# SyncE instead of GpSimd gathers the engines and clears the semaphores at the end of a decode kernel

## The chip, the cores and the metric

The kernel runs on one core of a Trainium2 chip. The metric is the device time of one execution in microseconds (us), as the median of several executions. "Relative to the copy" below means relative to the start of the last ScalarE instruction, which copies the finished output from PSUM; this takes the chance in the 379 us before it (some tenths of a microsecond from run to run) out of the comparison.

## The reference

One decode step of a gated mixture: grouped-query attention over a cache of 65,536 positions, a gMLP mixer for one token, and a gate between them.

```python
g = sigmoid((x * gate_w).sum(-1, keepdims=True))      # x: (1, 1, 1024) bf16
# a: 32 query heads, 4 kv heads, k_cache and v_cache (1, 4, 65536, 128) bf16, projections wq and wo
# b: gelu(x @ w_in), split, layernorm of one half, product, @ w_out
out = g * a + (1 - g) * b
```

Only the size matters to what follows: 162 MB must be read from HBM once, and the output is 2 KB.

## The kernel before

The body streams the caches through SBUF. The change does not touch it. What it touches is a function that rewrites the program's last block when the program is finished. The language's standard ending is a barrier of all engines, a clear of the kernel's semaphores by GpSimd, and a second barrier. The function had already cut this down to one gathering. After it the block is, engine by engine:

```text
TensorE, VectorE, ScalarE, SyncE:  drain, add 1 to the gather semaphore (96)
GpSimd:  five waits for two semaphores each (all loads and all engines' work done)
         drain (with an eleventh wait); wait until the gather is 4, subtract 4; drain; clear semaphores 100 to 111; drain
SyncE (after its own drain):  wait until the output has landed (semaphore 99 >= 32), subtract 32
```

The code that does it, cut:

```python
if engine == mybir.EngineType.Pool:
    drop += [l[2][0], l[6][0], l[7][0]]
    closer, gather = l[0][0], l[1][2]          # closer: the drain that gets the waits
    continue
...                                            # SyncE's waits are taken to hand them to closer
drop += [l[1][0], l[2][0]]
if engine == mybir.EngineType.SP:
    closed = l[3][0]                           # SyncE's last wait: for the output
else:
    drop.append(l[3][0])
...
block.instructions[closer] = copy.replace(
    block.instructions[closer],
    sync_info=mybir.SyncInfo(on_wait=list(waits.values()), on_update=[]))
```

The output itself is copied by ScalarE and written in two halves, one issued by ScalarE and one by SyncE:

```python
nc.scalar.copy(out=out_sb[:], in_=out_ps[:])
for i, queue in enumerate((nc.scalar, nc.sync)):
    p0 = (2 * i + 1) * B - 1
    ins = queue.dma_start(out=out_rows[2 * i:2 * i + 2, :], in_=out_sb[p0:p0 + 2, :])
    out_queues.append(ins.ins.name)
```

Of the kernel before, what the change touches and what calls it, by code (L numbers as in the profile page):

```python
# [29 lines left out]
def kernel(  # L30
# [90 lines left out]
    def close_with_one_barrier(n):  # L121
        block = n.main_func.blocks[-1]
        by = {}
        for i, ins in enumerate(block.instructions):
            by.setdefault(ins.engine, []).append((i, type(ins).__name__, ins))
        drop = []
        waits = None
        for engine, l in by.items():
            kinds = [k for _, k, _ in l]
            if engine == mybir.EngineType.Pool:  # L130
                assert kinds == ["InstDrain", "InstEventSemaphore", "InstEventSemaphore",
                                 "InstDrain", "InstISA", "InstDrain", "InstEventSemaphore",
                                 "InstEventSemaphore"]
                drop += [l[2][0], l[6][0], l[7][0]]
                closer, gather = l[0][0], l[1][2]
                continue
            if engine == mybir.EngineType.SP:
                assert l[0][2].has_wait() and not l[0][2].has_update()
                waits = list(l[0][2].sync_info.on_wait)
                drop.append(l[0][0])  # L140
                l, kinds = l[1:], kinds[1:]
            assert kinds == ["InstDrain", "InstEventSemaphore"] * 2
            drop += [l[1][0], l[2][0]]
            if engine == mybir.EngineType.SP:
                closed = l[3][0]
            else:
                drop.append(l[3][0])
        waits = {w.id: w for w in waits}
        total = 0
        for b in n.main_func.blocks:  # L150
            for i, ins in enumerate(b.instructions):
                if ins.name in out_queues:
                    u, = ins.sync_info.on_update
                    w = waits[u.id]
                    waits[u.id] = copy.replace(w, wait_value=w.wait_value - u.update_value)
                    total += u.update_value
                    b.instructions[i] = copy.replace(ins, sync_info=mybir.SyncInfo(
                        on_wait=ins.sync_info.on_wait,
                        on_update=[copy.replace(u, id=landed.num, ant_name=landed.name)]))
# [3 lines that stand above are left out]
        w, u = gather.sync_info.on_wait[0], gather.sync_info.on_update[0]  # L163
        block.instructions[closed] = copy.replace(
            block.instructions[closed],
            sync_info=mybir.SyncInfo(
                on_wait=[copy.replace(w, id=landed.num, ant_name=landed.name, wait_value=total)],
                on_update=[copy.replace(u, id=landed.num, ant_name=landed.name,
                                        update_value=total)]))
        for i in sorted(drop, reverse=True):  # L170
            del block.instructions[i]

    nc.at_finalize(close_with_one_barrier)

    kv = big.tile([P, NKV * CT * P], BF16, name="kv")
# [377 lines left out]
# [3 lines that stand above are left out]
# [40 lines left out]
```

## Time and profile before

| | |
|---|---|
| time, median of 3 runs | 382.19 us (382.17 to 382.25) |
| span of the profile, first to last instruction | 380.65 us |
| DMA busy, HBM rate over the span | 99%, 426 GB/s |
| start of the output copy to the end of the span | 1.73 us |
| end of the span to the end of the time | 1.51 us |

The page of the profile: busy time by engine, the busy share of 40 slices (9 is 90% or more), and the start of the chain that ended last.

```profile
PE 233.2 (61%) x1395; PEld 56.0 (15%) x800; DVE 218.5 (57%) x211; ACT 39.6 (10%) x55; POOL 4.4 (1%) x10
...
POOL 4000000000000000000000000000000000000000
...
DMA  9998999999999999999999999999999999999995
...
DMA 57%; PE 26%; DVE 13%; ACT 2%; issue 1%; SPq 1%; DVEq 0%; ACTq 0%
```

Only the first slice of GpSimd (POOL) has work: its set-up. DMA is full in nearly every slice but the last, whose 9.5 us hold the tail. So the kernel's length is set by the stream of loads, and an edit of the ending can change only the last two or three microseconds.

The tail by time (start us, duration us, engine, line, operation):

```profile
378.58 0.29 PE L506 MATMUL out_ps<-kv,oa 128*32 128x256 bf16 x4 [0.35 <-DMA kv<-in_A_wo_dram]
...
378.92 0.37 ACT L552 CAST out_sb<-out_ps 128x256 bf16<-128x256 f32 x1 [45.10 <-PE out_ps L506]
379.32 0.32 SPq L555 DMA_DIRECT2D out_dram<-out_sb  x1
379.32 0.25 ACTq L555 DMA_DIRECT2D out_dram<-out_sb  x1
```

The timeline stops here because waits, drains and clears are not counted as work. They appear when one asks for the line of the program's end. These are its groups before (line, engine, operation, count: duration in ns min/median/max, first and last start in us):

```profile
L591 POOLq EVENT_SEMAPHORE  x6: 17/43/682, 376.0 to 379.9; - x6
L591 POOLq DRAIN  x3: 34/41/72, 379.4 to 380.2; - x3
...
L591 SPq DRAIN  x1: 174/174/174, 379.7 to 379.7; - x1
L591 POOLq EVENT_SEMAPHORE_RANGE_CLEAR  x1: 96/96/96, 380.1 to 380.1; - x1
L591 SPq EVENT_SEMAPHORE  x1: 17/17/17, 380.6 to 380.6; - x1
```

GpSimd gathers and clears between 379.9 and 380.2, and SyncE's last wait stands at 380.6, when the output lands. Read like this, GpSimd looks hidden. But the time runs on for 1.51 us after the span. What happens there is in the trace's record of semaphore updates: the runtime's own end of a program. The Trainium skill, "Runtime: NRT & Kernel Launch", section "The ~15µs preamble/postamble breakdown", describes it: a barrier, then each engine resets 51 semaphores, then a barrier again; for the barrier at the start it also gives the pass, through the five engines and back. The trace agrees, and shows that pass at the end too. Semaphore 2 is raised nine times, semaphores up to 255 are reset in five blocks side by side, and semaphore 2 is raised nine times more:

```text
before: raises of semaphore 2, us from the span's start
first barrier   379.178 380.015 380.758 380.802 380.825 | 380.922 380.961 380.995 381.042
second barrier  381.919 381.953 381.992 382.035 382.058 | 382.157 382.195 382.229 382.276
```

The nine are five engines in a fixed order and then four on the way back, each waiting for the one before it. The ninth raise releases the block of resets that ends last (semaphores 51 to 101). So what moves the ninth raise moves the end. The reported time (382.16 us in this profile) is the distance from the last such raise at the start of the program to the sixth raise of the second barrier: 382.161 us.

### The profile page before, as it was taken

The numbers are of one execution on the slowest core, as the hardware profiler recorded it, in microseconds if no ns is written. First come the engines' busy times: TensorE is split into PE (matmuls) and PEld (weight loads), VectorE is DVE, ScalarE is ACT, GpSimd is POOL, SyncE is SP. The second block draws the span as 40 slices with busy tenths as digits, with TensorE's granted clock in tenths as the row PEclk, the third lists the DMA queues.
The fourth block names the chain that finished last, engine by engine and source line by source line (L and its number), as shares of the span: only waits on it lengthen the run. The fifth ranks groups of instructions, "written<-read, shape, count | busy, mean of one in ns | idle before, by whom it ended". The sixth has DMA issues, their size and how long they took to land.

```text
span 380.7 us, 2605 instructions
## 1 busy us (share of the span) xinstructions
PE 233.2 (61%) x1395; PEld 56.0 (15%) x800; DVE 218.5 (57%) x211; ACT 39.6 (10%) x55; POOL 4.4 (1%) x10
## 2 busy tenths in 40 slices
PE   0060657876157944796397729871977196839386
PEld 0010101111101210111011101120211011202113
DVE  4133288997597506966977059669970388460040
ACT  1001001110601100114010001050100000500000
POOL 4000000000000000000000000000000000000000
PEclk9995769899759895989688958895989579969789
DMA  9998999999999999999999999999999999999995
GB/s 386 496 420 379 411 438 441 437 483 430 387 420 441 441 436 441 427 441 441 434 436 441 441 427 434 406 423 441 434 434 429 420 441 442 436 410 430 424 443 223
DMA packets 3943, 162.17 MB, mean 426 GB/s; under 512 B 472, under 2 KB 476, under 8 KB 860
## 3 DMA queue, kind: packets, MB, share of 16 engines
q1 hardware_dynamic: 3892, 162.01, 98.8%
q8 instruction: 8, 0.13, 0.1%
q14 instruction: 3, 0.02, 0.0%
q10 hardware_dynamic: 40, 0.01, 0.0%
HBM read 162.01 MB, written 0.00 MB: 426 GB/s over the span
## 4 chain that ended last, share of the span: by engine, by line
DMA 57%; PE 26%; DVE 13%; ACT 2%; issue 1%; SPq 1%; DVEq 0%; ACTq 0%
DMA kv<-in_A_k_cache_dram 43%; PE s_ps L410 21%; DMA kv<-in_A_wo_dram 7%; DVE kv L403 7%; DMA kv<-in_A_v_cache_dram 7%; PE o_ps L456 4%; DVE pt L446 2%; DVE o_sb L470 1%; DVE mx L405 1%; ACT sc L421 1%; ACT sc L443 1%; DVE rowt L466 1%; SPq L184 1%; PE om_ps L476 0%; DVE osum L486 0%
## 5 line engine op out<-in xcount | busy, mean ns | idle before, releaser
L410 PE MATMUL s_ps<-kv,wt 128*128 128x512 bf16 x512 | 141.8, 437 | 80.2 <-DVE kv L403 80.2
L403 DVE STREAM_TRANSPOSE kv<-kv 128x2048 int32<-128x2048 int32 x64 | 142.7, 2281 | 54.3 <-DMA kv<-in_A_k_cache_dram 54.3
L456 PE MATMUL o_ps<-kv,pt 128*64 128x512 bf16 x512 | 61.7, 400 | 7.6 <-DMA kv<-in_A_v_cache_dram 7.6
L410 PEld LDWEIGHTS <-wt 128*128 128x128 bf16 x256 | 27.6, 108 | 195.6 <-issue 138.5
L421 ACT CAST sc<-s_ps 128x1024 bf16<-128x1024 f32 x16 | 16.2, 1012 | 249.9 <-PE s_ps L410 249.9
L456 PEld LDWEIGHTS <-pt 128*64 128x64 bf16 x256 | 16.1, 115 | 50.6 <-issue 48.1
L446 DVE STREAM_TRANSPOSE pt<-sc 128x1024 bf16<-128x1024 bf16 x16 | 18.6, 1217 | 6.8 <-ACT sc L443 6.8
L405 DVE TENSOR_REDUCE mx<-sc 128x1 f32<-128x1024 bf16 x12 | 14.5, 1210 | 9.9 <-ACT sc L421 9.9
L443 ACT ACTIVATE sc<-sc,nb 128x1024 bf16<-128x1024 bf16 x16 | 18.2, 1137 | 12.3 <-DVE nb L439 12.2
L466 DVE TENSOR_TENSOR rowt<-o_ps,own 128x1024 f32<-128x1024 f32 x4 | 4.8, 1195 | 24.9 <-PE o_ps L456 24.9
L476 PE MATMUL om_ps<-o_sb,hsel 128*32 128x128 f32 x8 | 2.3, 386 | 18.3 <-DVE o_sb L470 18.3
L425 DVE TENSOR_REDUCE mx<-sc 128x1 f32<-128x1024 bf16 x4 | 4.9, 1220 | 13.6 <-ACT sc L421 13.6
L296 PE MATMUL q_ps<-kv,xT 128*32 128x512 bf16 x64 | 5.6, 527 | 7.2 <-DMA kv<-in_A_wq_dram 7.2
L252 PE MATMUL xb_ps<-xg,spread 8*128 8x256 bf16 x1 | 0.4, 366 | 13.2 <-DMA xg<-in_gate_w_dram 13.2
L470 DVE TENSOR_REDUCE o_sb<-rowt 128x128 f32<-128x1024 f32 x4 | 7.5, 1872 | 0.1
L363 DVE TENSOR_TENSOR rowt<-q_ps,own_b 128x512 f32<-128x512 f32 x2 | 1.3, 686 | 10.8 <-PE q_ps L296 10.8
L296 PE MATMUL z_ps<-kv,xT 128*32 128x448 bf16 x64 | 5.9, 560 | 0.0
L495 PE MATMUL busy_ps<-wt 128*128 128x512 bf16 x23 | 5.8, 381 | 0.1
L506 PE MATMUL out_ps<-kv,oa 128*32 128x256 bf16 x128 | 4.2, 274 | 2.0 <-DMA kv<-in_A_wo_dram 2.0
L256 DVE TENSOR_TENSOR xm<-xb_ps,sel_i 128x128 f32<-128x128 f32 x2 | 0.5, 287 | 8.0 <-PE xb_ps L252 8.0
L552 ACT CAST out_sb<-out_ps 128x256 bf16<-128x256 f32 x1 | 0.4, 372 | 45.1 <-PE out_ps L506 45.1
L296 PEld LDWEIGHTS <-xT 128*32 128x32 bf16 x64 | 2.6, 136 | 14.6 <-issue 14.6
(90 smaller groups left out, 59.3 us busy)
## 6 DMA issues: line engine op xcount, KB each, us to landing
kv<-in_A_k_cache_dram SPq DMA_DIRECT2D x4, 4096.0 KB, 35.4
kv<-in_A_v_cache_dram SPq DMA_DIRECT2D x2, 4096.0 KB, 26.0
kv<-in_B_w_in_dram SPq DMA_DIRECT2D x1, 7168.0 KB, 19.4
kv<-in_A_wo_dram SPq DMA_DIRECT2D x1, 6144.0 KB
kv<-in_B_w_out_dram SPq DMA_DIRECT2D x1, 3584.0 KB
kv<-in_A_wo_dram SPq DMA_DIRECT2D x1, 1024.0 KB
kv<-in_A_wo_dram SPq DMA_DIRECT2D x1, 512.0 KB
kv<-in_A_wo_dram SPq DMA_DIRECT2D x2, 256.0 KB, 28.2
```

The costliest lines, as they stand in the source:

```text
L296: ins = nc.tensor.matmul(ps[t * B:(t + 1) * B, k * HN:k * HN + n], lhsT=xT[:, i * KH + c:i * KH + c + 1].to_broadcast([P, B]), rhs=w[:, c, ...
L403: nc.vector.transpose(out=kb[:, v * n:(v + 1) * n], in_=kb[:, v * n:(v + 1) * n])
L405: nc.vector.reduce_max(**late.pop())
L410: ins = nc.tensor.matmul(s_ps[:, k * HN:(k + 1) * HN], lhsT=wt[g % 2][:, v, b].rearrange("p a v h -> p (a v h)"), rhs=kx[:, b // 2, b % 2, ...
L421: nc.scalar.copy(out=sct[g, j][:], in_=s_ps[:])
L425: nc.vector.reduce_max(**late.pop())
L443: nc.scalar.activation(out=sct[g, j][:], in_=sct[g, j][:], func=ACT.Exp, scale=SCALE, bias=nb[:, 0:1], accum_out=lss[g][:, j:j + 1])
L446: nc.vector.transpose(out=ptt[g, j][:].rearrange("p c x -> p (c x)"), in_=sct[g, j][:])
L456: ins = nc.tensor.matmul(o_ps[g][hs, e, :], lhsT=ptt[g, j][:, 2 * u:2 * u + 2, :].rearrange("p c x -> p (c x)"), rhs=vx[:, 2 * u + e], sta ...
L466: nc.vector.tensor_tensor(out=om8, in0=o_ps[g][:].rearrange("p e (v d) -> p (e v) d", d=DH), in1=own_8[:].unsqueeze(2).to_broadcast([P, 2 ...
L470: nc.vector.tensor_reduce(out=o_sb[:], in_=om8.rearrange("p x d -> p d x"), axis=AX.X, op=ALU.add)
L495: ins = nc.tensor.matmul(ps[:, :HN], lhsT=w[:, :P], rhs=w[:, :HN], start=True, stop=True, skip_group_check=True)
```

## The change

The intent: GpSimd shall have nothing to do after its set-up, and SyncE, which must wait for the output anyway, shall gather and clear meanwhile. GpSimd's whole list of the last block and SyncE's are exchanged, and the closing wait for the output stays on SyncE.

```diff
-                drop += [l[2][0], l[6][0], l[7][0]]
-                closer, gather = l[0][0], l[1][2]
+                drop += [l[2][0], l[6][0]]
+                closer, gather, closed = l[0][0], l[1][2], l[7][0]
                 continue
...
-            drop += [l[1][0], l[2][0]]
-            if engine == mybir.EngineType.SP:
-                closed = l[3][0]
-            else:
-                drop.append(l[3][0])
+            drop += [l[1][0], l[2][0], l[3][0]]
...
         for i in sorted(drop, reverse=True):
             del block.instructions[i]
+        swap = {mybir.EngineType.Pool: mybir.EngineType.SP,
+                mybir.EngineType.SP: mybir.EngineType.Pool}
+        for i, ins in enumerate(block.instructions):
+            if ins.engine in swap:
+                block.instructions[i] = copy.replace(ins, engine=swap[ins.engine])
```

## The prediction

> **What bounds the kernel.** The page's slices show the DMA engines 90% or more busy in nearly all of the 380.7 us span, at 426 GB/s for 162 MB; the chain of waits is 57% DMA. None of that is touched: the instruction order before the last block is the same on every engine. Only what follows the last matmul can change.
>
> **That tail, from the records of single instructions and semaphore updates (us from the span's start).** Output copy on ScalarE 378.92 to 379.30; SyncE issues its half of the output 379.32 to 379.64; last landing of the output 380.62; SyncE's closing wait ends 380.65 and ends the span. GpSimd runs beside it: last semaphore wait 378.65 to 379.33, drain, gather of the engines 379.89, drain (72 ns), range clear (380.08, 96 ns), drain ending 380.23. Gather and clear are hidden behind the 0.98 us landing, with 0.4 us to spare.
>
> **What follows the span.** The Trainium skill, "Runtime: NRT & Kernel Launch", section "The ~15µs preamble/postamble breakdown", describes a barrier that passes over the five engines and back, about 44 ns a hop, then 51 semaphores reset by each engine, then a barrier again. The trace agrees: semaphore 2 is raised at 379.18, 380.02, 380.76, 380.80, 380.83, then four times to 381.04; resets to 381.60; nine more updates to 382.28. From the order in which the engines start after the first barrier I read the order TensorE, ScalarE, GpSimd, VectorE, SyncE. Then GpSimd, the third, comes 0.52 us after its last drain, while ScalarE needs 0.16 and TensorE 0.24. The next two hops, 44 and 23 ns, are as long as where everybody already waits, so SyncE was there by 380.80, under 0.15 us after its 380.65. GpSimd's slow exit therefore decides the end of the program now, by 0.02 to 0.07 us over SyncE.
>
> **What the change does.** GpSimd keeps one drain that adds to the gather and leaves the kernel at about 5 us; its 0.52 us exit goes off the path. SyncE gets, after its output issue, five semaphore waits, a drain, the gather, a drain, the range clear and a drain before its closing wait. Estimate from SyncE's own records (17 to 28 ns a wait, about 45 ns between instructions, clear 96 ns as on GpSimd): waits 379.69 to 380.05, gather done about 380.20, clear and drain by 380.45 to 380.55. The landing at 380.62 still ends the closing wait at 380.65. So 0.9 us of work moves onto SyncE, under a wait that it sat through anyway, with 0.1 us of slack.
>
> **Result.** The fifth step of the barrier goes from 380.83 to about 380.78: 0.05 us gained. If SyncE's chain overruns the landing by 0.1 us, 0.05 to 0.1 us is lost. Both are near the spread of the three runs (0.08 us), far below 2%. Predicted: 382.14 us, 8 in 10 between 381.9 and 382.4; faster by over 2% 0.005, within 2% 0.99, slower by over 2% 0.005.
>
> **Right or wrong would show as:** SyncE's closing wait ends within 0.04 us of the last landing, about 1.3 us after the output issue began; the range clear on SyncE ends before that landing; the third step of the end barrier follows ScalarE's by about 0.04 us instead of 0.74, and the fifth follows SyncE's wait by 0.10 to 0.15 us; the middle of the kernel is the same slice by slice.
>
> **What would make it wrong:** a drain on SyncE that sits until its output write is finished, a range clear much slower on SyncE, a slow exit that belongs to whoever cleared the semaphores rather than to GpSimd (then about 0.4 us lost), or a DMA stream at another rate.

## The result, and the profile after

| | before | after |
|---|---|---|
| time, median of 6 runs each | 382.18 us (381.99 to 382.25) | 382.11 us (382.10 to 382.28) |
| ratio after/before | | 1.000, 95% interval 0.9987 to 1.0013 |

The ratio is the mean time of one kernel's runs over that of the other's in the same rounds, so it is not quite the ratio of the medians. The verdict is "same", and the difference of the medians, 0.07 us, is smaller than the spread of either kernel.

The page after, the lines that answer to those above:

```profile
PE 232.1 (61%) x1397; PEld 55.6 (15%) x800; DVE 218.5 (57%) x211; ACT 39.6 (10%) x55; POOL 4.4 (1%) x10
...
DMA  9998999999999999999999999999999999999995
...
DMA 57%; PE 24%; DVE 15%; issue 2%; ACT 2%; SPq 1%; DVEq 0%; ACTq 0%
```

The body is as it was. The tail by time, after:

```profile
379.05 0.37 ACT L553 CAST out_sb<-out_ps 128x256 bf16<-128x256 f32 x1 [45.48 <-PE out_ps L507]
379.44 0.32 SPq L556 DMA_DIRECT2D out_dram<-out_sb  x1
379.45 0.26 ACTq L556 DMA_DIRECT2D out_dram<-out_sb  x1
```

The copy started 0.12 us later than in the profile before. That is the load stream's chance, and it is why the span is longer after (380.78 us against 380.65); whatever the change gains lies after the span. The groups of the program's end, after:

```profile
L592 SPq EVENT_SEMAPHORE  x7: 17/28/28, 379.8 to 380.8; - x7
L592 SPq DRAIN  x3: 7/7/7, 380.1 to 380.4; - x3
L592 POOLq DRAIN  x1: 4111/4111/4111, 1.0 to 1.0; - x1
...
L592 SPq EVENT_SEMAPHORE_RANGE_CLEAR  x1: 48/48/48, 380.3 to 380.3; - x1
```

GpSimd's only instruction of the ending starts at 1.0 us and is over with the set-up. SyncE does the rest: the clear at 380.31 takes 48 ns (96 on GpSimd), its drains 7 ns each (34 to 72 on GpSimd), and the last drain ends at 380.39. The output lands at 380.75 and SyncE's closing wait ends at 380.78. So SyncE did all of GpSimd's work in 0.58 us and still sat idle for 0.36 us.

The raises of semaphore 2 in the first barrier, relative to the copy. "Again" are the repeats described in the next section:

```text
               1      2      3      4      5   |  6      7      8      9      end of SyncE's wait
before         0.255  1.092  1.835  1.879  1.902  1.999  2.038  2.072  2.119   1.730
before again   0.254  1.096  1.839  1.884  1.907  2.004  2.044  2.078  2.124   1.732
after          0.256  1.097  1.135  1.179  1.866  1.910  1.949  1.984  2.031   1.738
after again    0.254  1.091  1.130  1.174  1.856  1.900  1.938  1.972  2.019   1.728
```

Before, the third raise, GpSimd's, comes 0.52 us after its last drain (1.311), and the fourth and fifth follow it at once. After, the third follows the second at once, and the fifth waits for SyncE alone. The end of SyncE's wait did not move. The gain at the fifth raise is 0.04 to 0.05 us, as predicted. But the sixth follows the fifth after 0.044 us instead of 0.097, so the ninth comes 0.10 us earlier (mean of the two before, 2.122, less that of the two after, 2.025). The prediction did not have that second part.

### The profile page after: what moved, and what is told of

Its sections match the earlier page's. It is cut to its first block, busy times and chain, and to the rows that moved or that the text cites. A ratio compares the mean times of both kernels' runs of the same rounds, so it can differ in the third digit from the quotient of the medians.

```text
span 380.8 us, 2607 instructions
## 1 busy us (share of the span) xinstructions
PE 232.1 (61%) x1397; PEld 55.6 (15%) x800; DVE 218.5 (57%) x211; ACT 39.6 (10%) x55; POOL 4.4 (1%) x10
## 4 chain that ended last, share of the span: by engine, by line
DMA 57%; PE 24%; DVE 15%; issue 2%; ACT 2%; SPq 1%; DVEq 0%; ACTq 0%
DMA kv<-in_A_k_cache_dram 42%; PE s_ps L411 19%; DVE kv L404 8%; DMA kv<-in_A_wo_dram 7%; DMA kv<-in_A_v_cache_dram 7%; PE o_ps L457 4%; DVE pt L447 2%; DVE mx L406 1%; DVE o_sb L471 1%; ACT sc L422 1%; ACT sc L444 1%; DVE rowt L467 1%; SPq L185 1%; PE om_ps L477 0%; DVE osum L487 0%
## 5 line engine op out<-in xcount | busy, mean ns | idle before, releaser
L411 PE MATMUL s_ps<-kv,wt 128*128 128x512 bf16 x512 | 139.8, 431 | 81.6 <-DVE kv L404 81.5
```

The costliest lines, as they stand in the source:

```text
L411: ins = nc.tensor.matmul(s_ps[:, k * HN:(k + 1) * HN], lhsT=wt[g % 2][:, v, b].rearrange("p a v h -> p (a v h)"), rhs=kx[:, b // 2, b % 2, ...
```

## The experiments

The theory: the program ends when the last engine has left for the runtime's barrier. Before, that was GpSimd, because it needs half a microsecond to leave. The change takes this off the path and puts work where SyncE has slack under the landing. Rivals: the difference of the medians is nothing but the spread; the slow exit belongs to whoever clears; or something else that SyncE does now made the gain.

Twelve kernels ran, all correct, in three groups of four on three chips. "Time minus span" needs each run's time and span only, so it exists for every run and not just for the profiled one (spans are given to 0.1 us, so one value is good to 0.05 us).

### Both kernels again

No edit.

> The kernel before, unchanged, to see what is repeatable. Theory (GpSimd's exit of 0.52 us decides the end of the program): the time is again 1.51 us longer than the span, third step of the end barrier 0.52 us after GpSimd's last drain, about 0.1 us after SyncE's closing wait. Rival (all of the difference between the two kernels is the spread of runs): time minus span lies anywhere between 1.3 and 1.5.

> The changed kernel, unchanged. Theory: time minus span 1.33 us again in every run, some 0.15 to 0.2 us less than before; SyncE's closing wait ends 0.02 to 0.04 us after the last landing; range clear over about 0.35 us before the landing. Rival (spread of runs): time minus span mixes with that of before; the ratio of the medians is within 0.0005 of 1 with either sign.

Before again: 382.25 us median of 5; after again: 382.22; the other kernel-before runs of the same rounds: 382.33 (9 runs). The ratio of after again to before is 0.9998, interval 0.9985 to 1.001. The total time cannot tell them apart. Time minus span can: 1.41 to 1.51, mean 1.44, in the 14 runs of before on this chip; 1.32 to 1.42, mean 1.35, in the 5 of after. (The changed kernel's six runs of the result give 1.28 to 1.41, mean 1.32; before gives means of 1.43 and 1.44 on the two other chips.) The raises above repeat within 0.012 us. So the gain of 0.09 to 0.10 us is real and is 0.025% of the time.

Two expectations were missed. Before again had 1.42 in its profiled run and not 1.51, and the changed kernel is 0.09 us below before in this measure, not 0.15 to 0.2. The missing 0.09 us was chance: in the first profile of before the second barrier's first raise came 0.315 us after the last reset. Eleven of the fourteen profiles have 0.224 or 0.225 there, and three have 0.315, two of them of variants of the changed kernel. The first pair of profiles therefore showed twice the true gain.

### VectorE clears

```diff
+        swap = {mybir.EngineType.Pool: mybir.EngineType.DVE,
+                mybir.EngineType.DVE: mybir.EngineType.Pool}
+        for i, ins in enumerate(block.instructions):
+            if ins.engine in swap:
+                block.instructions[i] = copy.replace(ins, engine=swap[ins.engine])
```

(in the kernel before; SyncE keeps its drain and closing wait)

> VectorE, idle at the end, gathers and clears in GpSimd's place; SyncE only waits for the output as before. Theory (the gain is GpSimd's leaving early; it doesn't matter who clears as long as it is done before the landing): same as the changed kernel, time minus span 1.33 us, VectorE's step of the barrier well before 380.8. Rival (a slow exit belongs to whoever clears): VectorE leaves 0.5 us after its last drain and time minus span stays at 1.5.

The time was 382.31 us median (382.04 to 382.38), not distinguishable from the others; time minus span 1.36 on average, as after. The groups of its end:

```profile
L596 DVEq EVENT_SEMAPHORE  x6: 21/50/672, 376.1 to 380.0; - x6
...
L596 POOLq DRAIN  x1: 4111/4111/4111, 1.0 to 1.0; - x1
...
L596 DVEq EVENT_SEMAPHORE_RANGE_CLEAR  x1: 114/114/114, 380.1 to 380.1; - x1
```

VectorE's clear is even slower than GpSimd's (114 ns). Yet its raise, the fourth, came at 1.402, 0.131 us after its last drain (1.271), and the ninth at 2.038, as in the changed kernel. A slow exit does not belong to whoever clears. It also shows that the fourth raise is VectorE's.

### GpSimd waits for the output

```diff
+        closed_name = block.instructions[closed].name
...
-            if ins.engine in swap:
+            if ins.engine in swap and ins.name != closed_name:
```

(in the changed kernel; SyncE still gathers and clears)

> As the changed kernel, but the closing wait for the output alone is put on GpSimd; SyncE gathers and clears. Theory (GpSimd needs about 0.5 us to leave, whatever it did last): the third step of the end barrier comes 0.5 us after the closing wait, time minus span (whose end is the wait's) becomes about 1.33 + 0.5 - 0.13 + 0.1 = 1.8 us, the total 0.4 us longer than the changed kernel. Rival (the clear made the exit slow, not the engine): GpSimd leaves within 0.15 us and the total is within 0.1 us of the changed kernel.

The time was 382.76 us median (382.58 to 382.84), 0.54 above after again on the same chip; no run of either kernel on that chip was as slow as its fastest. (The ratio to the runs of before is 1.001, interval 0.9998 to 1.0023; the mechanism is read from the raises.) Time minus span is 1.90 on average. The groups:

```profile
L593 SPq EVENT_SEMAPHORE_RANGE_CLEAR  x1: 47/47/47, 380.5 to 380.5; - x1
L593 POOLq EVENT_SEMAPHORE  x1: 17/17/17, 380.9 to 380.9; - x1
```

GpSimd cleared nothing here. Its one late instruction is a wait of 17 ns, ending 1.740 after the start of the copy. The third raise came at 2.307, 0.567 us later, and all later ones moved with it. GpSimd's exit is slow by itself, and the third raise is GpSimd's.

### GpSimd leaves a little earlier, and nothing is moved

```diff
-                drop += [l[2][0], l[6][0], l[7][0]]
+                drop += [l[i][0] for i in range(2, 8)]
```

(in the kernel before: no clear and no drains around it)

> The kernel before with GpSimd's range clear and the two drains around it left out (the trace shows the runtime resetting these semaphores itself): GpSimd ends with the gather, 0.3 us earlier, and nothing is moved to SyncE. Theory (only the moment matters at which GpSimd leaves): third raise 1.5 us after the start of the output copy, so SyncE decides: fifth at 1.86, ninth at 2.02, the same as the changed kernel. Rival (the gain came from something else that SyncE's taking over did): ninth raise stays at 2.12.

The time was 382.19 us median (382.06 to 382.32), against 382.29 for before on the same chip (ratio 0.9995, interval 0.998 to 1.001). Raises three, five, six and nine: 1.552, 1.874, 1.917, 2.037. From the fifth raise on this is the changed kernel's ending within 0.02 us, without the change. Leaving 0.32 us earlier (last instruction 0.991 instead of 1.311) was enough, because SyncE then decides. So a reader who wants only this gain need not move anything. The output was correct in every run; the trace has semaphores 100 to 111 reset by the runtime's own pass, 2.10 to 2.37 us after the start of the copy. Whether that can be relied on elsewhere was not tested.

### How much slack: more waits on GpSimd, more waits on SyncE

```diff
-            sync_info=mybir.SyncInfo(on_wait=list(waits.values()), on_update=[]))
+            sync_info=mybir.SyncInfo(on_wait=list(waits.values()) * 2, on_update=[]))
```

(or `* 3`, `* 4`; the build splits the list into waits for two semaphores each; all are true by then but the one for the output copy)

> The kernel before with the list of closing waits doubled (all are long true): 9 instead of none of the two-semaphore waits follow the output copy on GpSimd, about 0.087 us each. Theory (GpSimd is the last to leave, without slack): its last drain ends 0.78 us later, 2.09 us after the start of the output copy, and the ninth raise of semaphore 2 (TensorE released) comes at about 2.90 us instead of 2.12; time up by 0.75 to 0.8 us. Rival (GpSimd is hidden and SyncE's wait for the landing decides): no change.

> The changed kernel with the same doubling, now on SyncE: 6 more waits of about 0.063 us after the output issue. Theory (SyncE has 0.36 us of slack under the landing): the last drain moves from 1.35 to 1.73 us after the start of the output copy, just past the landing at 1.70; ninth raise at 2.03 to 2.09 us instead of 2.02: time up by at most 0.07 us, where the same edit cost the kernel before 0.78. Rival (work on SyncE is on the path): up by 0.38 us.

> Three times the waits on SyncE: 11 more, 0.69 us. Theory: past the slack of 0.36 us the cost is one for one: last drain at 2.04, closing wait ends at about 2.10 instead of 1.73 us after the start of the output copy, ninth raise at 2.40; time up by 0.35 to 0.4 us, and the closing wait no longer waits. Rival (off the path altogether): no change.

> The changed kernel with four times the waits on SyncE: 16 more than it has, 5 more than with three times. Theory (past the slack, one for one, 0.061 us a wait): the last drain ends at 2.35 to 2.40 us after the start of the output copy (2.05 with three times), ninth raise at about 2.74 (2.43). The time with three times rose by 0.26 us more than the raises show. If that part is a fixed step it stays 0.26 here, and the time is 383.15 to 383.2; if it grows with the instructions it is about 0.38.

> The kernel before with three times the waits: 11 of 0.087 us after the copy instead of 9 with twice. Corrected theory (GpSimd sat 0.4 us at the gather for SyncE's drain; past that slack one for one): its last drain ends 0.17 us later than with twice, 1.87 us after the start of the output copy, ninth raise at 2.68 (2.51 with twice, 2.12 without). Rival (the first theory, no slack: 0.087 for each added wait, 0.96): 3.08.

| kernel | waits added after the copy or issue | last drain of the clearing engine | ninth raise | time, median |
|---|---|---|---|---|
| before (again) | | 1.315 | 2.124 | 382.25 |
| before, twice | 9 on GpSimd | 1.698 | 2.507 | 382.65 |
| before, three times | 11 on GpSimd | 1.834 | 2.644 | 382.76 |
| after (again) | | 1.347 | 2.019 | 382.22 |
| after, twice | 6 on SyncE | 1.705 | 2.063 | 382.19 |
| after, three times | 11 on SyncE | 2.052 | 2.434 | 382.87 |
| after, four times | 17 on SyncE | 2.423 | 3.296 | 383.33 |

(Raises and drains in us relative to the copy. The rows come from three chips, so the medians compare roughly; before read 382.22 to 382.33 in the three groups.)

Read it in three steps. First, twice the waits moved the last drain by about as much in both kernels, 0.38 us on GpSimd and 0.36 on SyncE. In the kernel before the ninth raise moved with it by 0.38; in the changed kernel it moved by 0.04. That contrast is the change's whole content: after its last drain GpSimd was on the path, and SyncE had room. Second, the expectation for before was 0.78 and half of it was wrong. The records say why: GpSimd arrives at the gather about 0.43 us before SyncE's drain has let it pass, so it had slack there, just not after it: its drain before the gather moved by 0.82 us with twice the waits, and 0.38 came through. (The same edit adds about twice as much work on GpSimd as on SyncE, so the costs alone, without the drains, would not be a fair comparison.) The corrected expectation for three times (2.68, against 3.08 without slack) was met with 2.644. Third, on SyncE the cost starts where the room ends, with the closing wait at 1.773 and 2.120 instead of 1.728. The groups of the changed kernel with three times the waits:

```profile
L592 SPq EVENT_SEMAPHORE  x18: 17/28/28, 379.9 to 381.2; - x18
...
L592 SPq EVENT_SEMAPHORE_RANGE_CLEAR  x1: 52/52/52, 381.1 to 381.1; - x1
```

The output landed at 380.82 in that run, so the clear at 381.1 and the closing wait at 381.2 come after it: the last wait no longer waits.

Four times was a miss. One line of its groups:

```profile
L592 SPq EVENT_SEMAPHORE  x24: 17/28/28, 379.7 to 381.4; - x24
```

The expectation counted 16 added waits; the profile has 24 semaphore instructions on SyncE at the end against 7 in the changed kernel, so 17 were added, 6 more than with three times. Six of 0.061 us put the last drain at 2.42, and it was 2.423. Its closing wait ended at 2.485, but the fifth raise came 0.648 us after that wait instead of 0.128: that the cost goes on one for one was wrong here. And three times had already cost more time than its raises show: the reported time is 0.26 us longer than the distance between the two raises with which it agrees elsewhere. Whether the extra lies at the start or at the end of the time, the profile does not show.

### The same number of waits, placed where SyncE is idle

```diff
-                        on_wait=ins.sync_info.on_wait,
+                        on_wait=ins.sync_info.on_wait if ins.engine != mybir.EngineType.SP else
+                        [x for x in ins.sync_info.on_wait if "Activation" not in x.ant_name] * 23
+                        + [x for x in ins.sync_info.on_wait if "Activation" in x.ant_name],
```

(in the changed kernel: 11 more waits on SyncE ahead of its output issue)

> The changed kernel with 11 more waits on SyncE, as many as three times the list added, but placed where SyncE sits idle for 28 us before it issues its half of the output; the last wait before the issue is one instruction longer, so up to 0.06 us on the path. If SyncE's number of instructions alone makes the unexplained 0.26 us (its stream is longer), the time minus span rises from 1.35 to about 1.6 here too with no shift of the ninth raise; if it comes with work after the output issue, it stays at 1.35 and the time at 382.2 to 382.3.

Nothing but a few hundredths moved on the path: ninth raise 2.043. Yet time minus span rose to 1.61 on average (1.55 to 1.70), and the reported time was again 0.259 us longer than the distance between the raises, the same as with three times the waits. So that part is not made by work after the issue. In these runs it goes with the number of instructions added on SyncE, but not evenly: 6 more give 0.02, 11 more give 0.26 whether early or late, and 17 more give 0.12 there and 0.52 at SyncE's exit (one profile each). The time (382.40 us median) has a ratio of 1.0003 to before, unresolved. What this part is stays open. The Trainium skill, "Runtime: NRT & Kernel Launch", section "Instruction fetch mechanics", says that a branch out of the fetched window stalls until the target page has come. That would fit an effect that depends on where the stream ends, but it is not shown. The trace records instruction fetches as DMA packets, and the tail has one in a single run, the one with 17 more: 8 KB, from 3.550 to 3.884 us after the start of the copy. That is after the late fifth raise (3.133), and the two runs with 0.259 have none.

### One transfer for the output

```diff
-    for i, queue in enumerate((nc.scalar, nc.sync)):
-        p0 = (2 * i + 1) * B - 1
-        ins = queue.dma_start(out=out_rows[2 * i:2 * i + 2, :], in_=out_sb[p0:p0 + 2, :])
-        out_queues.append(ins.ins.name)
+    ins = nc.scalar.dma_start(out=out_rows[:, :], in_=out_sb[::B, :])
+    out_queues.append(ins.ins.name)
```

(in the changed kernel, to shorten the landing that now ends everything)

> The changed kernel with the output written by one transfer of four rows on ScalarE's queue; SyncE issues none. Theory (in the changed kernel the landing of the output ends everything): the last landing decides still; if SyncE's longer issue (0.32 against 0.26 us) is what makes the last landing late, it comes 0.05 to 0.17 us earlier and the ninth raise at 1.85 to 1.98 instead of 2.02; SyncE's clear ends by 1.2 us and is off the path. Rival (one queue with four rows takes longer to issue): landing later than 1.70, ninth raise after 2.02. In time at most 0.2 us either way.

The rival of the expectation was right, and more so than stated. The timeline:

```profile
378.92 0.37 ACT L553 CAST out_sb<-out_ps 128x256 bf16<-128x256 f32 x1 [44.85 <-PE out_ps L507]
379.33 0.61 ACTq L554 DMA_DIRECT2D out_dram<-out_sb  x1
```

The one issue of four rows takes 0.61 us where each half takes 0.25 or 0.32 side by side. The landing comes at 2.076 instead of 1.70 and the ninth raise at 2.400: 0.38 us later than the changed kernel, almost double the "at most 0.2" that was expected of the time. In the time itself it is 382.36 against 382.22 for before on that chip, unresolved (ratio 1.0002, interval 0.999 to 1.0015). No version was found that beats both kernels by a margin that the time resolves.

## Why the prediction was right

- **The time and the range.** Predicted 382.14 us, 381.9 to 382.4, within 2%; measured 382.11. Right. Chance in the load stream (0.1 us and more between runs) is as large as the whole effect, so the median alone would not prove the reasons, and that it came within 0.03 us is luck.
- **"GpSimd's slow exit therefore decides the end of the program now, by 0.02 to 0.07 us over SyncE."** Right. With SyncE's exit of 0.128 us, as the changed kernel's profile shows it, SyncE would have come to the barrier at 380.78 before, 0.044 us ahead of the actual fifth raise at 380.83. (In the runs without the clear and with the clear on VectorE, which leave SyncE's ending as it was before, SyncE's exit took 0.142 and 0.141; with these it is 0.03 us.) That the exit is GpSimd's and not the clear's is shown by the VectorE run (exit 0.131 with the clear) and by the run in which GpSimd waits for the output (exit 0.567 without it).
- **"0.9 us of work moves onto SyncE, ... with 0.1 us of slack."** The sign was right and the sizes were off. SyncE took 0.58 us: the five waits 0.28 where 0.36 had been estimated, the drain and gather 0.11 against 0.15, and the drain, clear and drain 0.19 against 0.25 to 0.35 (the clear 48 ns where 96 had been assumed). So its slack was 0.36 us. The runs with more waits confirm it: 6 waits of 0.06 us used it up at a cost of 0.04, and 11 overran it by about the expected amount (ninth raise 2.434, expected 2.40).
- **"0.05 us gained."** The mechanism was right and the sum lacked a term. The fifth raise gained 0.04 to 0.05 as predicted. The return from the fifth to the sixth raise fell from 0.097 to 0.044 us in addition. It is 0.097 or 0.098 in all five profiles where VectorE's own raise came 0.02 us before the fifth, and 0.043 to 0.045 in all nine where VectorE had raised at least 0.28 us earlier. Going by SyncE's exit, these are also just the profiles in which SyncE came to the barrier before its turn (the five) or last (the nine), so which of the two sets the turn is not separated. The gain is 0.10 us.
- **The signs named beforehand** all appeared: closing wait 0.034 us after the landing, clear over before the landing, third raise 0.038 us after ScalarE's, fifth 0.128 us after SyncE's wait. The slices of DMA are equal digit by digit, and those of the engines differ by a tenth at most.
- **What was not seen:** that GpSimd had 0.43 us of slack at the gather before, waiting for SyncE's drain (which made the first expectation for doubled waits twice too large), and that SyncE's exit is not a constant: with 17 more instructions on SyncE it rose from 0.128 to 0.648 us.

## What to carry to other kernels

In these runs the program ended when the slowest engine had reached the runtime's barrier, not when the span of the profile ended, so add each engine's exit to the end of its last instruction before calling it hidden: here about 0.55 us for GpSimd and 0.13 to 0.15 us for SyncE and VectorE. Here the engine that waited for the output's landing anyway did the closing work for nothing, because its 0.58 us fitted under that wait with 0.36 to spare; measure the room by adding known waits until the raises move. This ending was worth a tenth of a microsecond, which only relative readings of the trace resolved: in a kernel of 382 us the time is "same", and a single pair of profiles doubled the true gain by chance.

## What the Trainium skill lacked or had wrong

- "Runtime: NRT & Kernel Launch", section "The ~15µs preamble/postamble breakdown", gives about 355 ns for the pass of the barrier at the start, as 44 ns a hop for 8 hops. The sum is about right: the runs show 370 to 372 ns at the start and 356 to 358 in the second barrier at the end. The page does not say how unequal the hops are: 23 to 50 ns for most, but 111 to 113 ns for the turn from the fifth to the sixth raise at the start and 97 to 99 at the end, or 43 to 45 there when SyncE came last and the fourth engine long before it.
- The same section gives about 1.5 us for the barrier at the end, as a wait for all engines. It does not say how long each engine takes from its last instruction to its raise: 0.52 to 0.57 us on GpSimd, 0.13 on VectorE, 0.16 on ScalarE, 0.13 to 0.15 on SyncE, but 0.65 when SyncE's stream was 17 instructions longer.
- "VectorE: DVE Perf Modes", section "The DRAIN you can't avoid", gives about 12 ns for the drains that the runtime adds. It has nothing on drains that the program itself writes at its end. On SyncE those took 7 ns, though its output transfer had not landed, and 164 to 174 ns where the drain came just after the issue and added to the gather; on VectorE 10 to 17 ns, and on GpSimd 34 to 72 ns.
